# The last half block of a fused attention and MLP kernel: one copy and one store become two of each, on two engines and two queues

## The chip, the cores and the metric

The kernel runs on one core of a Trainium2 chip. The metric is the device time of one execution in microseconds; the median of several executions counts, and lower is better.

## The reference

A state of 32 rows and a sequence of 512 rows attend to each other for each of 8 batches and 8 heads. Both results are joined along the rows, the heads along the columns, and the 4352 rows go through a two-layer MLP with a leaky ReLU.

```python
def _attn_ref(x, state):                      # x 8x8x512x64, state 8x8x32x64
    scores = scale * np.matmul(x, state.transpose(0, 1, 3, 2))
    a = softmax(scores)
    xread = np.matmul(a, state)
    scores2 = scale * np.matmul(state, x.transpose(0, 1, 3, 2))
    a2 = softmax(scores2)
    sread = np.matmul(a2, x)
    return np.concatenate([xread, sread], axis=2)

def _moe_ref(x, w_in, w_out):                 # x 4352x512, w_in 512x2048, w_out 2048x512
    h = x @ w_in
    g = np.maximum(0.01 * h, h)
    return g @ w_out
```

(`softmax` stands here for the written-out maximum, exponential, sum and division of the original.) Inputs and output are fp32; the kernel multiplies in bf16 and accumulates in fp32.

## The kernel before

The kernel works batch by batch. For each batch it computes scores and probabilities, and it folds the state into the first weight matrix, so that the first MLP layer of a batch is one product of probabilities (`aT`) and the folded weights (`M`), 16 blocks of 128 hidden columns for 512 rows (`ff1`, line 429). The second layer is a product of 512 rows x 2048 with 2048 x 512. From batch 2 on, and for half of batch 1, it is done in blocks by a scheme of seven block products instead of eight: sums and differences of blocks are formed on DVE and POOL (`s_sum`, `tw_sum`), and `product` (line 605) multiplies them on TensorE. A block result has 256 rows (two halves of 128, `v` = 0 and 1) and 256 output columns (`HN`).

The products of a batch are normally spread over the next batch's first layer. For the last batch, 7, there is no next one, and its products are written out by hand at the end (lines 1234 to 1276), interleaved with the MLP of the state's rows (`f_product`, `two_product`). The order of the instructions on each engine is that of the source: the pools and the wait placement are automatic, the schedule is manual.

The end of the program is this. After the state rows' last product their results go out in eight stores of 32 rows each, four issued from SP and four from ACT (line 1266). Then product 3 of batch 7 (line 1270), its sum on DVE (`y_add`, line 729) and its store from SP (`y_pair`, line 735). Last comes product 4 in two halves (line 1274): for each half eight matmuls of 128 x 256, which add to what products 1, 6 and 7 left. The two halves lie in two different PSUM tiles (`ppw`, 256 fp32 columns of each are used). The first half is copied to the output tile `ysb` on DVE and the second on ACT (line 1275), and each is stored by SP (line 1276) as 128 rows of 256 fp32 columns, 128 KB. `rows_of(b)[2 + v]` picks every fourth row of the batch's 512 output rows, so each of the 128 rows is a piece of 1 KB in DRAM.

What stands at line 1302 in the profile is the program's closing: SP waits for the completion semaphores of all DMAs, and then the engines meet in a barrier.

Of the kernel before, what the change touches and what calls it, by code (L numbers as in the profile page):

```python
# [9 lines left out]
P = 128  # L10
# [17 lines left out]
def kernel(  # L28
# [9 lines left out]
    nc = tc.nc  # L38
# [14 lines left out]
    VEC, SCA, POO = nc.vector.tensor_copy, nc.scalar.copy, nc.gpsimd.tensor_copy  # L53
# [496 lines left out]
    HN = DM // 2  # L550
# [27 lines left out]
    hTs, sums, prods = {}, {}, {}  # L578
# [26 lines left out]
    def product(b, n, v, j0=0, j1=8):  # L605
        q = prods.setdefault(b, {})
        bank = "x" if n in (1, 6, 7, 4) else "b"
        first = n in (1, 2, 5) and v == 0 and j0 == 0
        if first:
            if b == B - 1 and n == 1:  # L610
                ts = [psum.tile([P, 2, DM], FP32, name="ppw", tag=t, bufs=1) for t in ("sc", "big")]
                q[bank] = [t[:, 0, :HN] for t in ts]
                q["whole", bank] = None
            else:
                t = psum.tile([P, 2, HN], FP32, name=f"pp{bank}", tag="py")
                q[bank] = [t[:, u] for u in range(2)]
                q["whole", bank] = t[:]
        wide = b == B - 1 and n == 1
        q["open", bank] = first or (wide and j0 == 0)
        at = slice(P * v, P * (v + 1))  # L620
        low = slice(HN * 1 + P * v, HN * 1 + P * (v + 1))
        for j in range(j0, j1):
            lhsT = {
                1: lambda: hTs[b][:, j, at],
                2: lambda: hTs[b][:, HJ + j, at],
                4: lambda: hTs[b][:, HJ + j, low],
                3: lambda: sums[b, 4][:, j, at],
                5: lambda: sums[b, 1][:, j, at],
                6: lambda: sums[b, 2][:, j, at],
                7: lambda: sums[b, 3][:, j, at],  # L630
            }[n]()
            nc.tensor.matmul(  # L632
                q[bank][v], lhsT=lhsT, rhs=w_of(n, j), start=q["open", bank] and j == 0,
                stop=j == 7, skip_group_check=True,
            )
# [82 lines left out]
    def y_block(b, u, c):  # L718
        q = prods[b]
        if ("y", u) not in q:  # L720
            q["y", u] = ypool.tile([P, 2, DM], FP32, name="ysb", tag="ysb")
        return q["y", u][:, :, HN * c:HN * (c + 1)]
# [35 lines left out]
    def rows_of(b):  # L758
        return out[b * SROW:b * SROW + S, :].rearrange("(p t) f -> t p f", t=NT)
# [474 lines left out]
    b = B - 1  # L1234
# [37 lines left out]
    y_pair(b, 0, HN, DM)  # L1272
    for v in range(2):
        product(b, 4, v)
        (VEC, SCA)[v](y_block(b, 1, 0)[:, v], prods[b]["x"][v])
        nc.sync.dma_start(rows_of(b)[2 + v][:, :HN], y_block(b, 1, 0)[:, v])


# [28 lines left out]
```

## Time and profile before

| What | us |
|---|---|
| Runs: 202.83, 203.06, 203.06; median | 203.06 |
| Time of the profiled execution | 202.94 |
| Its span, first to last instruction | 201.1 |
| TensorE busy in the span | 194.1 |
| Granted TensorE clock | 1.000 |
| DVE copy of the first half (line 1275), from 197.12 | 0.424 |
| ACT copy of the second half (line 1275), from 198.00 | 0.372 |
| SP's issues of the two last stores (line 1276), from 197.58 and 198.40 | 0.356, 0.345 |
| Last store of 128 KB, from issue to landing | 1.8 |

Times within the span count from its first instruction. PE is TensorE's matmuls, PEld its weight loads, SPq and ACTq the instruction queues of SP and ACT with their DMA issues; "landing" is the arrival of a DMA's completion semaphore. The median of the runs is 0.12 above the profiled execution, whose time holds 1.8 us outside the span.

### The profile page before, as it was taken

To read this page: it belongs to the slowest core of one execution; us is meant where nothing else is said; L and a number is where in the kernel's file an instruction comes from. 1 tells how busy PE (TensorE), PEld (TensorE's weight loads), DVE (VectorE), ACT (ScalarE), POOL (GpSimd) and SP (SyncE) were. 2 spreads that over 40 slices of the span, in tenths; PEclk is the share of its full clock that TensorE was granted. 3 is DMA by queue.
4 is the path that set the end of the run, shared out by engine and by line. 5 is a ranking of instruction groups with operands and counts; after the bars stand their busy time and mean duration, and the time that the engine had idled before them with its cause. 6 is when DMAs were issued, how large, how long until landed. Compare 5 with 4: busy or idle time off the path is not lost.

```text
span 201.1 us, 4590 instructions
## 1 busy us (share of the span) xinstructions
PE 194.1 (96%) x1853; PEld 129.4 (64%) x1880; DVE 161.7 (80%) x243; ACT 143.5 (71%) x273; POOL 62.3 (31%) x67
## 2 busy tenths in 40 slices
PE   6999999999999999999999999999999999999993
PEld 2643534443476767766776677676767777799982
DVE  2866799899998999889987999697999945984712
ACT  3679677888989878777777878777868555757420
POOL 8734180030190274017500670054004600540000
PEclk9999999999999999999999999999999999999999
DMA  6999999896999737843293505220025202210115
GB/s 197 207 206 297 255 261 175 142 345 128 231 220 204 273 46 52 259 197 74 42 265 118 155 3 104 106 108 0 0 100 160 56 3 103 108 47 10 52 37 171
DMA packets 38773, 27.75 MB, mean 138 GB/s; under 512 B 24416, under 2 KB 35808, under 8 KB 38752
## 3 DMA queue, kind: packets, MB, share of 16 engines
q1 hardware_dynamic: 33584, 20.78, 40.7%
q0 software_dynamic: 4832, 6.29, 15.4%
q10 hardware_dynamic: 336, 0.39, 0.8%
q8 instruction: 14, 0.23, 0.5%
q14 instruction: 7, 0.06, 0.1%
HBM read 17.30 MB, written 8.91 MB: 130 GB/s over the span
## 4 chain that ended last, share of the span: by engine, by line
PE 75%; DMA 14%; DVE 3%; ACT 2%; POOL 2%; issue 1%; ACTq 1%; POOLq 0%
PE ph L432 20%; PE ppx L632 18%; PE ppb L632 16%; DMA w_out_bf<-in_moe_w_out_dram 8%; PE ppr L689 6%; DMA w_in_bf<-in_moe_w_in_dram 5%; PE py L537 3%; PE pf L510 3%; PE pm L411 3%; PE ppw L632 3%; PE psr L384 2%; PE pyw L537 2%; DVE tw L576 1%; DMA out_dram<-ysb 1%; POOL w_in_bf L145 1%
## 5 line engine op out<-in xcount | busy, mean ns | idle before, releaser
L437 ACT ACTIVATE hT<-ph 128x512 bf16<-128x512 f32 x112 | 66.4, 603 | 24.0 <-PE ph L432 20.6
L432 PE MATMUL ph<-aT,M 128*128 128x512 bf16 x201 | 60.6, 379 | 0.3
L597 POOL TENSOR_TENSOR S<-hT,S 128x512 bf16<-128x512 bf16 x24 | 32.1, 1359 | 83.1 <-DVE S L597 66.9
L632 PEld LDWEIGHTS <-S 128*128 128x128 bf16 x384 | 37.2, 98 | 12.7 <-issue 0.2
L632 PEld LDWEIGHTS <-hT 128*128 128x128 bf16 x288 | 27.8, 98 | 11.7 <-issue 1.3
L597 DVE TENSOR_TENSOR S<-hT 128x1024 bf16<-128x1024 bf16 x24 | 25.3, 1078 | 2.4 <-ACT hT L437 2.4
L432 PEld LDWEIGHTS <-M 128*128 128x128 bf16 x224 | 20.9, 98 | 9.4 <-issue 3.7
L632 PE MATMUL ppx<-tw,S 128*128 128x256 bf16 x160 | 20.7, 273 | 0.2
L537 PEld LDWEIGHTS <-hT 128*128 128x128 bf16 x96 | 9.1, 98 | 11.6 <-issue 1.3
L537 PE MATMUL py<-w_out_bf,hT 128*128 128x512 bf16 x63 | 15.9, 379 | 0.2
L132 POOL CAST xb<-xl 128x2048 bf16<-128x2048 f32 x5 | 9.5, 1893 | 12.7 <-DMA xl<-in_x_dram 12.7
L425 ACT CAST M<-pm 128x1024 bf16<-128x1024 f32 x12 | 12.2, 1016 | 0.6 <-PE pm L411 0.6
L632 PE MATMUL ppb<-tw,S 128*128 128x256 bf16 x96 | 12.4, 273 | 0.2
L632 PE MATMUL ppb<-w_out_bf,hT 128*128 128x256 bf16 x96 | 12.5, 273 | 0.1
L729 DVE TENSOR_TENSOR ysb<-ppb,s 128x512 f32<-128x512 f32 x12 | 8.3, 688 | 5.3 <-PE ppb L632 5.3
L632 PE MATMUL ppb<-w_out_bf,S 128*128 128x256 bf16 x96 | 12.3, 273 | 0.2
L632 PE MATMUL ppx<-w_out_bf,hT 128*128 128x256 bf16 x80 | 11.2, 273 | 0.1
L337 ACT ACTIVATE e<-sc,mcol 128x512 bf16<-128x512 f32 x16 | 11.1, 697 | 0.0
L632 PE MATMUL ppx<-tw,hT 128*128 128x256 bf16 x80 | 10.4, 273 | 0.1
L289 DVE TRANSPOSE_TENSOR_REDUCE r<-e 128x32 f32<-128x1024 bf16 x7 | 8.7, 1242 | 1.6 <-ACT e L284 1.5
L331 DVE TENSOR_REDUCE mcol<-sc 128x2 f32<-128x1024 f32 x8 | 9.7, 1215 | 0.0
L266 DVE TRANSPOSE_TENSOR_REDUCE mrow<-sc 128x32 f32<-128x1024 f32 x7 | 8.7, 1243 | 0.5 <-PE sc L256 0.5
(150 smaller groups left out, 313.0 us busy)
## 6 DMA issues: line engine op xcount, KB each, us to landing
out_dram<-ysb SPq DMA_DIRECT2D x11, 512.0 KB, 2.6
xl<-in_x_dram SPq DMA_DIRECT2D x5, 1024.0 KB, 6.4
out_dram<-ysb SPq DMA_DIRECT2D x9, 256.0 KB, 4.6
w_in_bf<-in_moe_w_in_dram POOLq DMA_DIRECT2D x4, 512.0 KB, 9.4
xf<-in_x_dram SPq DMA_DIRECT2D x4, 256.0 KB, 3.7
w_out_bf<-in_moe_w_out_dram POOLq DMA_DIRECT2D x4, 256.0 KB, 13.6
x<-in_x_dram POOLq DMA_DIRECT2D x2, 512.0 KB, 14.4
w_out_bf<-in_moe_w_out_dram POOLq DMA_DIRECT2D x2, 512.0 KB, 15.4
```

The source lines that it names most:

```text
L132: nc.gpsimd.tensor_copy(xt[b][:].rearrange("p t h d -> p h t d"), xl[b][:].rearrange("p h (t d) -> p h t d", t=NT),)
L266: nc.vector.tensor_reduce(out=m1[:], in_=flat.rearrange("p (c j) -> p c j", j=NS), axis=AX.X, op=ALU.max, apply_transpose=True,)
L289: nc.vector.tensor_reduce(out=r1[:], in_=e1[:].rearrange("p (c j) -> p c j", j=NS), axis=AX.X, op=ALU.add, apply_transpose=True,)
L331: nc.vector.tensor_reduce(out=a.m2[:], in_=a.sc[:], axis=AX.X, op=ALU.max, negate=True)
L337: nc.scalar.activation(out=a.e2[:, g], in_=a.sc[:, g, :], func=AF.Exp, bias=a.m2[:, g:g + 1], accum_out=a.r2[:, g:g + 1],)
L425: copy(a.M[:, :, cols], pm[:])
L432: nc.tensor.matmul(ph[:], lhsT=a.M[:, g, P * j:P * (j + 1)], rhs=a.aT[:, g, :], start=(g == 0), stop=(g == 1),)
L437: nc.scalar.activation(out=hT[:, j, :], in_=ph[:], func=AF.Prelu, scale=1 / SCALE, alpha=0.01)
L537: nc.tensor.matmul(y.py, lhsT=hT[:, j, P * i:P * (i + 1)], rhs=w_out_bf[:, j, :], start=(j == 0), stop=(j == 15),)
L597: eng.tensor_tensor(out=part(n), in0=in0, in1=in1, op=op)
L632: nc.tensor.matmul(q[bank][v], lhsT=lhsT, rhs=w_of(n, j), start=q["open", bank] and j == 0, stop=j == 7, skip_group_check=True,)
L689: nc.tensor.matmul(q.bank[w], lhsT=lhsT, rhs=w_of(n, j), start=n in (1, 2, 5) and j == 0, stop=j == HJ - 1, skip_group_check=True,)
```

## The change

The first half is treated as before: copied on DVE, stored from SP. The second half's 256 columns are divided: columns 0 to 127 are copied on DVE and stored from SP's queue, columns 128 to 255 are copied on ACT and stored from ACT's queue. Both parts are read from the same PSUM tile. Each store is 64 KB, 128 rows of 512 bytes. Nothing else is altered.

```diff
     for v in range(2):
         product(b, 4, v)
-        (VEC, SCA)[v](y_block(b, 1, 0)[:, v], prods[b]["x"][v])
-        nc.sync.dma_start(rows_of(b)[2 + v][:, :HN], y_block(b, 1, 0)[:, v])
+        y = y_block(b, 1, 0)[:, v]
+        parts = ((VEC, nc.sync, 0, P), (SCA, nc.scalar, P, HN)) if v else ((VEC, nc.sync, 0, HN),)
+        for copy, eng, c0, c1 in parts:
+            copy(y[:, c0:c1], prods[b]["x"][v][:, c0:c1])
+            eng.dma_start(rows_of(b)[2 + v][:, c0:c1], y[:, c0:c1])
```

## The prediction

> **What bounds the kernel now.** I read the page's first part and the chain of waits first. TensorE is busy for 96% of the span and the chain lies on it for three quarters.
>
> ```profile
> span 201.1 us, 4590 instructions
> PE 194.1 (96%) x1853; PEld 129.4 (64%) x1880; DVE 161.7 (80%) x243; ACT 143.5 (71%) x273; POOL 62.3 (31%) x67
> PE 75%; DMA 14%; DVE 3%; ACT 2%; POOL 2%; issue 1%; ACTq 1%; POOLq 0%
> ```
>
> The diff adds no matmul and moves none. Only the end after the last matmul can change, so the next view is the timeline of the last microseconds (start, length, engine, line).
>
> ```profile
> 196.05 1.91 PE L632 MATMUL ppw<-tw,hT 128*128 128x256 bf16 x16
> 196.97 0.39 SPq L735 DMA_DIRECT2D out_dram<-ysb  x1
> 197.12 0.42 DVE L1275 COPY ysb<-ppw 128x256 f32<-128x256 f32 x1 [0.18 <-PE ppw L632]
> 197.58 1.16 SPq L1276 DMA_DIRECT2D out_dram<-ysb  x2
> 198.00 0.37 ACT L1275 COPY ysb<-ppw 128x256 f32<-128x256 f32 x1 [3.12 <-DMA out_dram<-ysb]
> ```
>
> The last matmul ends at 196.05 + 1.91 = 197.96, ACT copies from 198.00 to 198.37, SP issues the last store at 198.40, and the span ends at 201.1. The row puts ACT's wait down to a store of the same moment, but the program's wait is for TensorE, which ended 0.04 before. So 3.1 us of tail follow the last product: 0.4 of copy, 2.7 behind the store's issue. The view of the issues by line and the view of SP's end-of-program instructions split the latter.
>
> ```profile
> L1276 SPq DMA_DIRECT2D out_dram<-ysb x2: 345/350/356, 197.6 to 198.4; - x2
> L1266 ACTq DMA_DIRECT2D out_dram<-ysb x4: 395/441/442, 194.9 to 196.3; - x4
> out_dram<-ysb ACTq DMA_DIRECT2D x4, 64.0 KB, 1.8
> out_dram<-ysb SPq DMA_DIRECT2D x1, 128.0 KB, 1.8
> L1302 SPq EVENT_SEMAPHORE  x9: 28/28/28, 198.8 to 200.2; - x9
> ```
>
> The last store lands 1.8 us after its issue began, at 198.40 + 1.83 = 200.23. SP then passes the last of nine wait instructions, which start at 198.8 to 200.2. These nine are the gate at the program's end: they wait one after another for every DMA semaphore. In narrow windows they start at 198.79, 198.86, 198.92, 198.98, 199.04, 199.33, 199.40, 199.81 and 200.25. The first five had nothing to wait for (their DMAs had landed) and still follow each other by 0.06 to 0.07, (199.04 - 198.79) / 4 = 0.064 us. The sixth, eighth and ninth wait for landings: the 256 KB store, the first 128 KB store, the last one. After the ninth, drains and the closing barrier take 201.13 - 200.25 = 0.88.
>
> **The copy.** The change takes away one ACT copy of 256 columns (0.372) and puts in a DVE and an ACT copy of 128 columns. No row has a DVE copy of 128 fp32 columns out of PSUM. DVE takes 0.424 for 256 and 0.692 for 512 (the row of line 547), so 0.268 per 256 columns and 0.424 - 0.134 = 0.290 for 128; bounds are 0.175 (the 128x16 row of line 831) and 0.424. ACT has a row of that size:
>
> ```profile
> L191 ACT CAST st<-pst x1: 272/272/272, 5.8 to 5.8; 128x128 bf16<-128x128 f32 x1
> ```
>
> The instruction list of the changed program decides how they stand to each other: the DVE copy waits for TensorE, the ACT copy waits for DVE's count after that copy, and not for TensorE. The two copies of one PSUM bank are in line, not at once. DVE is free (its copy of the first half ends at 197.55), so it runs from 198.00 to 198.29; a hand-over takes some 0.03 (TensorE's end at 197.96 to ACT's start at 198.00, ACT's end at 198.37 to SP's issue at 198.40); ACT runs from 198.32 to 198.59. Before, all 256 columns were out at 198.37: the split is 0.22 late.
>
> The Trainium skill, in PSUM — Partial Sum Buffer, section PSUM bank collisions raise a hardware error, holds that two engines may not access one bank and quadrant together, reads against reads included. By that rule the wait is needed; no run here shows a collision. Were the copies side by side, the sum below would be 0.3 smaller.
>
> **The stores.** The last store of 128 KB becomes two of 64 KB. SP's own (128 rows of 512 B) is issued after the DVE copy, at 198.32 and not 198.40, and is off the path. ACT's is issued after its copy, at 198.59 + 0.03 = 198.62. Nothing is queued on ACT behind it, and its queue has been empty since 198.03 (the fourth L1266 store, 196.30 + 1.73). ACT's issue takes 0.40 to 0.44 against SP's 0.35. The windows view gives the DMA engines a share of 0.91 at 198.50 to 199.00, 0.27 at 199.00 to 199.20, and 0.96 at 199.40 to 199.60 (the last store): they are free again when the new stores' packets come, from 199.2 on.
>
> How long does 64 KB in 512 B pieces take to land? No row has it. The nearest are ACT's four stores of 64 KB (2 KB pieces), 1.7 to 1.9, and SP's of 128 KB, 1.8. Half the bytes may save up to half of the 0.45 us in which the last store's packets ran; the longer issue costs 0.09. I take 1.8, with 1.6 (fastest L1266 store) and 2.0 (slowest) as bounds. ACT's half is landed at 200.42 (200.22 to 200.62), against 200.23 before.
>
> The Trainium skill, in DMA: Bandwidth & Descriptors, section Issuing engines are not separate DMA queues, says that issuing from two engines saves only the issuing time, since the transfers share the same DMA engines. By that rule the second queue could save 0.35 here at most. It saves 0.05, because ACT's store is ready at 198.62 and SP would be free at 198.32 + 0.35 = 198.67; ACT's longer issue takes that back.
>
> **The gate at the end.** This is the dearest term and the diff does not show it. Each DMA issued from SP or ACT takes the next of eight completion semaphores in turn, and SP's nine end waits go through these in their fixed order, the first instruction having none of them. Before, the last store had the eighth: it was the last thing SP waited for, and everything else was passed during its flight. One store more means that ACT's store takes the first semaphore. In the changed program's list the second of the nine instructions waits for it. SP reaches it at about 198.77, stands there until 200.42, and only then passes seven more, which have all landed (the first half's store, the latest other, stood at 199.81; SP's half lands near 198.32 + 1.8 = 200.12). Seven of them at 0.064 are 0.45. This cost is at most 0.48 (0.069 each) and at least nothing, if passed waits should run closer.
>
> **Sum.** Old end of the gate: 200.25. New: 200.42 + 0.015 (landing to passing, as before) + 0.45 = 200.88. The difference is +0.63: 0.22 from the later issue (198.62 for 198.40), less 0.03 of landing (1.80 for 1.83), plus 0.45 from the gate, rounded. What hid those seven waits was the last store's flight; that cover is gone. With landing 1.6 to 2.0 it is +0.43 to +0.83. The profiled execution took 202.94, 1.8 more than its span; that gives 203.57. The runs' median is 203.06 (202.83 to 203.06), which gives 203.69. I forecast 203.6, between the two.
>
> **Rivals.**
> *The gate costs nothing* (passed waits overlap): 203.06 + 0.18 = 203.2, no change. For it: each wait instruction is only 28 ns long. Against: the five passed waits before have the 0.064 spacing without anything to wait for. Chance 0.06.
> *The change does what it says*, and the copies run side by side: ACT ends at 198.27, its store lands at 198.30 + 1.8 = 200.10, and the gate ends at 200.57, +0.32: 203.35, read as no change. Against: the wait in the instruction list. Chance 0.04.
> *A store's time goes with its bytes* (the other side, not slower): the 64 KB land in half of 1.83, 0.92 after 198.62, at 199.54. Then ACT's store no longer ends last; SP passes the waits up to the seventh by 199.87, the first half's store having landed by 199.81, and the last at 200.12 at the latest, or below 200 if SP's half gains too: -0.15 to -0.35, 202.7 to 202.9. It decides once landing takes below 1.17 us. Against: the page's 64 KB stores take 1.6 to 2.0, as long as 128 KB. Chance 0.04, half of it read as faster by the scatter of the runs (202.83 to 203.06), half as no change.
> *The two last stores collide*: 512 B pieces run at the cost of larger ones and two queues share the engines, landing 2.0 or later as the slowest SP store did beside ACT's: +0.83 and more, 203.9. For it: the 32-row stores issued from both queues at once landed up to 0.4 apart. Against: the stores are issued 0.3 apart and each needs some 0.2 us of packets. Chance 0.07.
>
> **How the numbers follow.** The forecast has 0.79. A measurement of this kernel tells about 0.2%, 0.41 us, from no change. Some 0.04 of the forecast (landing at its short bound, or the scatter of 0.23 among the runs) reads as no change. Slower: 0.75 + 0.07 = 0.82; no change: 0.04 + 0.06 + 0.04 + 0.02 = 0.16; faster: 0.02. The range is the forecast's own bounds from the lowest run (202.83 + 0.43 = 203.26) to the median with the long landing (203.06 + 0.83 = 203.89), rounded out to 203.25 and 203.95; it takes in the second and the fourth rival.
>
> **What would show it.** In the changed profile the DVE copy starts at 198.0 and the ACT copy at 198.3, after it. Of SP's nine end waits one has started by 198.8, the second starts at 200.4 and the other seven follow within 0.45. If the ACT copy starts at 198.0, the copies are side by side; if the last wait starts within 0.1 of the landing of ACT's store, the gate term is wrong; if that store lands before 199.8, the landing is.

## The result and the profile after

The changed kernel takes 203.56 us (median of 14 runs, 203.20 to 204.49) against 203.06 (14 runs, 202.66 to 203.78): a ratio of 1.003 with a 95% interval of 1.0016 to 1.0044, so half a microsecond slower. One of the runs with one store more below (207.43 us) and two of those with four more (207.07 and 206.47) had a lower granted clock, 0.992, and are left out of the medians and ratios. The profiled execution took 203.46 with a span of 201.7; that of before took 202.94 with 201.1.

The page of the changed kernel, its first part:

```profile
span 201.7 us, 4620 instructions
PE 195.8 (97%) x1880; PEld 129.4 (64%) x1880; DVE 161.2 (80%) x244; ACT 143.2 (71%) x273; POOL 62.4 (31%) x67
```

TensorE shows 27 matmuls more only because the trace of before misses as many records (1853 against 1880 weight loads in both). The timeline of the end (start, length, engine, line, operation, and in brackets what the engine waited for):

```profile
196.13 1.91 PE L632 MATMUL ppw<-tw,hT 128*128 128x256 bf16 x16
197.66 1.08 SPq L1279 DMA_DIRECT2D out_dram<-ysb  x2
198.08 0.29 DVE L1278 COPY ysb<-ppw 128x128 f32<-128x128 f32 x1 [0.45 <-PE ppw L632]
198.40 0.27 ACT L1278 COPY ysb<-ppw 128x128 f32<-128x128 f32 x1 [3.44 <-DVE ysb L1278]
198.70 0.36 ACTq L1279 DMA_DIRECT2D out_dram<-ysb  x1
```

The last matmul ends at 198.04. The two copies run one after the other: ACT sat idle for 3.44 us and what ended the wait is DVE's copy of the other columns. Copying ends at 198.67, 0.63 after the last matmul; before it was 0.41. ACT issues its store at 198.70. The issues of the last three stores, with the median time from issue to landing:

```profile
out_dram<-ysb SPq DMA_DIRECT2D x1, 128.0 KB, 2.2
out_dram<-ysb SPq DMA_DIRECT2D x1, 64.0 KB, 1.7
out_dram<-ysb ACTq DMA_DIRECT2D x1, 64.0 KB, 1.7
```

So ACT's half is landed 1.65 later, at 200.35. Now the end waits of SP in the changed kernel, first in the view of what SP's queue waited for (total, times, longest), then its wait instructions up to that landing and behind it (count, shortest, median and longest in ns, first and last start):

```profile
SPq L1305 <- DMA out_dram<-ysb: 1.5, 1, 1.5
```

```profile
L1305 SPq EVENT_SEMAPHORE  x1: 17/17/17, 198.8 to 198.8; - x1
...
L1305 SPq EVENT_SEMAPHORE  x8: 28/28/28, 200.4 to 200.8; - x8
```

And the first of these views for the kernel before:

```profile
SPq L1302 <- DMA out_dram<-ysb: 1.0, 3, 0.4
```

Before, SP went through its nine waits while the stores landed, held up three times for 0.4 at most. After, it passes one wait, stands 1.5 us at the second, and then goes through eight (the one that held it and seven that had nothing to wait for) from 200.36 to 200.79. That walk of 0.43 us lies behind the last landing and in front of the closing barrier, which takes 0.88 in both kernels.

In the sections below all times of the tail count from the end of the last matmul, since that end itself moves from profile to profile (197.62 to 198.78 in the profiles read below of kernels with the matmuls of before). Two points matter: when the last store is landed, and when the last of SP's end waits starts.

| Kernel | last store issued | landed | last end wait |
|---|---|---|---|
| before | 0.43 | 2.27 | 2.29 |
| after | 0.66 | 2.31 | 2.75 |

The difference is 0.47 us: 0.22 from the later issue, -0.19 from the shorter landing, 0.43 from the gate. The span grew by 0.54, since the last matmul also ended 0.08 later in this profile.

### The profile page after: what moved, and what is told of

It reads as the page before. It is cut to its first block, busy times and chain, and to the rows that moved or that the text cites. A ratio compares the mean times of both kernels' runs of the same rounds, so it can differ in the third digit from the quotient of the medians.

```text
span 201.7 us, 4620 instructions
## 1 busy us (share of the span) xinstructions
PE 195.8 (97%) x1880; PEld 129.4 (64%) x1880; DVE 161.2 (80%) x244; ACT 143.2 (71%) x273; POOL 62.4 (31%) x67
## 4 chain that ended last, share of the span: by engine, by line
PE 78%; DMA 13%; DVE 4%; POOL 2%; ACT 1%; issue 0%; POOLq 0%; ACTq 0%
PE ph L432 22%; PE ppx L632 17%; PE ppb L632 16%; DMA w_out_bf<-in_moe_w_out_dram 8%; PE ppr L689 6%; DMA w_in_bf<-in_moe_w_in_dram 5%; PE ppw L632 3%; PE py L537 3%; PE pf L510 3%; PE pm L411 3%; PE psr L384 2%; PE pyw L537 2%; DVE tw L576 1%; POOL w_in_bf L145 1%; PE sc L256 1%; DVE sh L274 1%
## 5 line engine op out<-in xcount | busy, mean ns | idle before, releaser
L432 PE MATMUL ph<-aT,M 128*128 128x512 bf16 x224 | 65.3, 379 | 0.1
```

Source lines behind the costliest of these rows:

```text
L432: nc.tensor.matmul(ph[:], lhsT=a.M[:, g, P * j:P * (j + 1)], rhs=a.aT[:, g, :], start=(g == 0), stop=(g == 1),)
```

## The experiments

**One store more, nothing else.** From the kernel before; the store of batch 7's first block half is cut into two. The expectations put this store some 15 us ahead of the end; in the trace of before it is issued at 179.40, 21.7 ahead of it.

```diff
-            y_pair(b, 0, 0, HN)
+            for v in range(2):
+                nc.sync.dma_start(rows_of(b)[v][:, :HN], y_block(b, 0, 0)[:, v])
```

> The kernel before, with one store more about 15 us ahead of the end: the store of batch 7's first block half is cut into two. Copies and last stores are those of before; only the completion semaphores move on by one, so that the last store has the first of the eight. From the last matmul's end to the last of SP's end waits it is 2.29 us before and 2.75 after. Theory (the gate costs 7 waits of 0.062): 2.72, and a time 0.43 us over before's. Rival (the time was lost in the copies in line and the stores, the gate is free): 2.29 and before's time.

203.29 us against 202.90, a ratio of 1.0027 (1.0017 to 1.0037). The last store lands at 2.28, as before, and the last end wait starts at 2.73 (the theory said 2.72). SP's end waits in this kernel, the one ahead of the landing and those from it on:

```profile
L1303 SPq EVENT_SEMAPHORE  x1: 28/28/28, 198.4 to 198.4; - x1
...
L1303 SPq EVENT_SEMAPHORE  x8: 28/28/28, 199.9 to 200.3; - x8
```

It is the picture of the changed kernel, one wait and then eight, with the copies and the last stores of before. A store cut far from the end, with nothing else changed, brings the tail to 2.73 where the whole change brings it to 2.75.

**The changed kernel with the gate hidden again.** The same early store goes out from POOL, whose DMAs count on other semaphores; ACT's last store then has the eighth again.

```diff
-            y_pair(b, 0, 0, HN)
+            nc.gpsimd.dma_start(pair_rows(b, 0)[:, :, :HN], prods[b]["y", 0][:, :, :HN])
```

> The changed kernel, with the store of batch 7's first block half, some 15 us ahead of the end, issued from POOL instead of SP. POOL's stores count on other semaphores, so those of SP and ACT move back by one and ACT's last store has the eighth again. Copies in line and split stores stay. Theory: the gate's 0.43 us goes, last matmul to last end wait 2.75 - 0.43 = 2.32, time equal to before's within 0.1 us. Rival (gate free, copies and stores cost it all): 2.75 and still 0.5 us over before's.

202.97 us against 202.90, a ratio of 1.0003 (0.9993 to 1.0012). Landing at 2.31 as in the changed kernel, last end wait at 2.33 against its 2.75. All nine of SP's end waits, from the first to the last start, in one view:

```profile
L1305 SPq EVENT_SEMAPHORE  x9: 17/28/28, 198.8 to 200.4; - x9
```

With the gate hidden, the copies in line and the split store cost 0.04 us of tail over before, less than the runs can tell.

**The control for the moved store**: the same edit in the kernel before.

> The kernel before, with only the store of batch 7's first block half issued from POOL. The last store then has the seventh semaphore; one wait follows its own. It is the control for the runs in which this store was moved. Theory: 2.29 + 0.06 = 2.35, a time within 0.1 us of before's. Rival (the moved store itself is what brought the changed kernel back to before's time): clearly under before's time, by 0.2 us or more.

The last store lands at 2.27, SP passes it at 2.29, and the last end wait starts at 2.35, one step of 0.06 later. The time is 203.05 against 202.99, a ratio of 1.0019 (1.0007 to 1.0032). It is not under before's, so the move is not what brought the changed kernel back. That the ratio is more than 0.06 us would make is left open; the medians are 0.06 apart.

**Four stores more.** The early store cut into five, so that four waits follow the last store's.

```diff
-            y_pair(b, 0, 0, HN)
+            for i in range(5):
+                lo, hi = (0, 32, 64, 96, 112, 128)[i:i + 2]
+                nc.sync.dma_start(pair_rows(b, 0)[lo:hi, :, :HN], prods[b]["y", 0][lo:hi, :, :HN])
```

> The kernel before, with the store of batch 7's first block half, some 15 us ahead of the end, cut into five. The last store then has the fourth of the eight semaphores and four waits follow its own. Theory (each wait behind the last landing costs 0.062): last matmul to last end wait 2.29 + 0.25 = 2.54. Rival (one more wait behind it costs the same whatever the number): 2.72 as with seven; or nothing, 2.29.

203.36 us against 202.99, a ratio of 1.0016 (0.9998 to 1.0035). Its profiled execution is the one of 207.07 us, so the tail is read from another execution of the same kernel:

> The kernel with the store of batch 7's first block half cut into five, once more for its profile. Theory: the last store lands 2.27 after the last matmul, as before, and four waits of 0.06 follow: last matmul to last end wait 2.53. Rival (one more wait behind it costs the same whatever the number): 2.72.

It took 203.16 beside 203.25 before, which says nothing either way; the tail does. The last store lands at 2.32, 0.05 later than before's, and the last end wait starts at 2.58, 0.24 after SP passed the landing. SP's end waits from the landing on:

```profile
L1304 SPq EVENT_SEMAPHORE  x5: 28/28/28, 200.2 to 200.5; - x5
```

Five instructions, the one that waited and four that did not. The walk behind the landing is thus 0.06 for one wait (the control), 0.24 for four and 0.43 for seven: 0.061 each.

**One copy, two stores.** From the changed kernel; ACT copies all 256 columns of the last half, and both stores wait for that.

```diff
-        parts = ((VEC, nc.sync, 0, P), (SCA, nc.scalar, P, HN)) if v else ((VEC, nc.sync, 0, HN),)
-        for copy, eng, c0, c1 in parts:
-            copy(y[:, c0:c1], prods[b]["x"][v][:, c0:c1])
+        (VEC, SCA)[v](y, prods[b]["x"][v])
+        for eng, c0, c1 in ((nc.sync, 0, P), (nc.scalar, P, HN)) if v else ((nc.sync, 0, HN),):
             eng.dma_start(rows_of(b)[2 + v][:, c0:c1], y[:, c0:c1])
```

> The changed kernel, with the last half's 256 columns copied by ACT in one instruction as before, and the two stores of 64 KB kept, one from SP and one from ACT, both waiting for that copy. The gate is as in the changed kernel. Theory: both stores are issued 0.40 after ACT's start instead of 0.64, so last matmul to last end wait 2.75 - 0.22 = 2.53, a time 0.24 over before's. Rival (the copies in line cost nothing, because the two stores share the DMA engines and the pair lands as late as one of 128 KB): 2.29 + 0.43 = 2.72.

203.43 us against 202.90, a ratio of 1.0029 (1.0015 to 1.0043). The theory fell. The stores were issued at 0.44, 0.22 sooner than ACT's in the changed kernel, and the last end wait still started at 2.79, later than its 2.75 and past the rival's 2.72. The timeline of this kernel and its issues with their times to landing:

```profile
197.95 0.37 ACT L1276 COPY ysb<-ppw 128x256 f32<-128x256 f32 x1 [3.12 <-DMA out_dram<-ysb]
198.35 0.34 SPq L1278 DMA_DIRECT2D out_dram<-ysb  x1
198.35 0.37 ACTq L1278 DMA_DIRECT2D out_dram<-ysb  x1
```

```profile
out_dram<-ysb SPq DMA_DIRECT2D x1, 64.0 KB, 1.9
out_dram<-ysb ACTq DMA_DIRECT2D x1, 64.0 KB, 2.1
```

Issued together, the two halves land 1.9 and 2.1 after issue instead of 1.7 and 1.7 when they were 0.3 apart. SP's half has the first semaphore here, so the gate's walk of 0.43 starts at its landing, 2.35, and covers ACT's at 2.51.

**One copy, two stores, gate hidden**: the last edit and the store from POOL together.

> Both edits together: ACT copies 256 columns in one, two stores of 64 KB from two queues, and one earlier store issued from POOL, so that SP's last store has the eighth semaphore. Theory: the gate is hidden again and 64 KB land 0.17 sooner than 128 KB (1.67 for 1.84): last matmul to last end wait 2.29 - 0.17 = 2.12, a time 0.17 us under before's. Rival (stores issued together share the DMA engines and land as one of 128 KB): 2.29, before's time.

203.15 us against 202.90, a ratio of 1.0008 (0.9998 to 1.0018). It did not beat before: ACT's half landed at 2.46, and the last end wait started at 2.54, 0.25 later than before's. Here ACT's half has the seventh semaphore and SP's the eighth, so one wait of 0.06 still follows the last landing; the other 0.19 is the landing itself. Two stores of 64 KB at once are later than one of 128 KB (2.27).

**Half of it alone.** The run with one copy and two stores without SP's half: the left 128 columns of the last half are left out of the output.

```diff
-        for eng, c0, c1 in ((nc.sync, 0, P), (nc.scalar, P, HN)) if v else ((nc.sync, 0, HN),):
+        for eng, c0, c1 in ((nc.scalar, P, HN),) if v else ((nc.sync, 0, HN),):
```

> ACT copies the last half's 256 columns in one, and only the right 128 columns are stored, 64 KB from ACT; the left 128 columns of that half are left out of the output. ACT's store has the eighth semaphore. It is the run with one copy and two stores without SP's half. Theory (two stores issued together hold each other up): issued at 0.44 after the last matmul, landed 1.65 later, last matmul to last end wait 2.10. Rival (it is ACT's queue, or 512 B pieces, at that moment): 2.46 to 2.54 as with both.

It was run once, 202.75 us beside 202.97. The view of its last issues:

```profile
out_dram<-ysb SPq DMA_DIRECT2D x1, 128.0 KB, 2.2
out_dram<-ysb ACTq DMA_DIRECT2D x1, 64.0 KB, 1.6
```

The same store from the same queue, issued at the same 0.44, lands at 2.08 when SP's is not there, and at 2.46 to 2.51 when it is. It is the company that costs, not ACT's queue or the pieces of 512 B.

**Copies side by side.** From the changed kernel; the right 128 columns of the last half are accumulated in another PSUM tile.

```diff
-                q[bank] = [t[:, 0, :HN] for t in ts]
+                q[bank] = [ts[0][:, 0, :HN], [ts[1][:, 0, :P], ts[0][:, 1, :P]]]
...
-            nc.tensor.matmul(
-                q[bank][v], lhsT=lhsT, rhs=w_of(n, j), start=q["open", bank] and j == 0,
-                stop=j == 7, skip_group_check=True,
-            )
+            to, w = q[bank][v], w_of(n, j)
+            for p, r in zip(to, (w[:, :P], w[:, P:])) if isinstance(to, list) else ((to, w),):
+                nc.tensor.matmul(
+                    p, lhsT=lhsT, rhs=r, start=q["open", bank] and j == 0,
+                    stop=j == 7, skip_group_check=True,
+                )
...
```

The rest of the diff makes the readers of that half follow.

> The changed kernel, with the right 128 columns of the last half accumulated in another PSUM tile (matmuls of 128 columns for that half, 32 more in all, so TensorE works some us longer; only the tail is read). The ACT copy no longer waits for the DVE copy. ACT's store has the eighth semaphore and SP's the first, so the gate stays. Both copies start at 0.04 after the last matmul and both stores are issued at 0.34 to 0.36. Theory (two stores issued together land later, as in the run with one copy and two stores, 1.9 and 2.08 after issue): last matmul to last end wait 0.355 + 1.91 + 0.43 = 2.70, so that side by side copies gain only 0.05 on the changed kernel's 2.75. Rival (64 KB land 1.65 after issue, as ACT's store did in the changed kernel): 0.355 + 1.65 + 0.43 = 2.44, a gain of 0.31.

The time, 204.06 against 202.99, holds the 32 added matmuls and is not compared. The tail in the timeline, and the issues with their times to landing:

```profile
198.67 0.29 DVE L1281 COPY ysb<-ppw 128x128 f32<-128x128 f32 x1 [1.03 <-PE ppw L634]
198.73 0.27 ACT L1281 COPY ysb<-ppw 128x128 f32<-128x128 f32 x1 [3.76 <-DMA out_dram<-ysb]
198.99 0.35 SPq L1282 DMA_DIRECT2D out_dram<-ysb  x1
199.03 0.36 ACTq L1282 DMA_DIRECT2D out_dram<-ysb  x1
```

```profile
out_dram<-ysb SPq DMA_DIRECT2D x1, 64.0 KB, 1.8
out_dram<-ysb ACTq DMA_DIRECT2D x1, 64.0 KB, 1.9
```

ACT starts 0.06 after DVE, while DVE is still copying: the wait for DVE came from the shared PSUM tile. SP's half lands at 2.10 and ACT's at 2.27; the last end wait starts at 2.55, between the theory's 2.70 and the rival's 2.44. SP's end waits from its half's landing on:

```profile
L1308 SPq EVENT_SEMAPHORE  x8: 27/28/28, 200.8 to 201.2; - x8
```

That is 0.20 off the changed kernel's tail, but the copies are little of it. In this kernel SP's half has the first semaphore and ACT's the eighth, so the walk of 0.43 starts at SP's landing, 2.10, and covers ACT's. The later landing itself moved only from 2.31 to 2.27; an estimate from these rows for the changed kernel's order of waits is 2.27 + 0.02 + 0.43 = 2.72, only 0.03 off its 2.75. And 2.27 is also the landing of the single 128 KB store before. Even with copies side by side the store is not in sooner; the 0.1 us gained at the copy goes to two stores that hold each other up.

**The store cut by rows.** One ACT copy, 64 rows of 1 KB from SP and 64 from ACT, with the store from POOL. The edit is against the kernel before.

```diff
-            y_pair(b, 0, 0, HN)
+            nc.gpsimd.dma_start(pair_rows(b, 0)[:, :, :HN], prods[b]["y", 0][:, :, :HN])
...
-        (VEC, SCA)[v](y_block(b, 1, 0)[:, v], prods[b]["x"][v])
-        nc.sync.dma_start(rows_of(b)[2 + v][:, :HN], y_block(b, 1, 0)[:, v])
+        y = y_block(b, 1, 0)[:, v]
+        (VEC, SCA)[v](y, prods[b]["x"][v])
+        for eng, p0, p1 in ((nc.sync, 0, 64), (nc.scalar, 64, P)) if v else ((nc.sync, 0, P),):
+            eng.dma_start(rows_of(b)[2 + v][p0:p1, :HN], y[p0:p1])
```

> One ACT copy of 256 columns as before, its store divided by rows and not by columns: 64 rows of 1 KB from SP and 64 from ACT, issued together, and the earlier store from POOL, so that the gate is hidden. Half as many pieces as with the cut by columns. Theory (two stores issued together land late, whatever their pieces): last matmul to last end wait 2.45 to 2.54, as with the cut by columns (2.54). Rival (the 512 B pieces are what costs): 2.27 or less, a time equal to before's or under it.

203.56 us against 202.99, a ratio of 1.003 (1.0012 to 1.0048), and neither expectation held: the last end wait started at 2.97. Each issue took 0.56 to 0.58 instead of 0.35, and the halves landed 2.2 and 2.5 after it. So one half was tried by itself, from the kernel before; the last half's other 64 rows are left out of the output.

```diff
-        (VEC, SCA)[v](y_block(b, 1, 0)[:, v], prods[b]["x"][v])
-        nc.sync.dma_start(rows_of(b)[2 + v][:, :HN], y_block(b, 1, 0)[:, v])
+        y = y_block(b, 1, 0)[:, v]
+        (VEC, SCA)[v](y, prods[b]["x"][v])
+        for p1 in (64,) if v else (P,):
+            nc.sync.dma_start(rows_of(b)[2 + v][:p1, :HN], y[:p1])
```

> The kernel before, with only the first 64 of the last half's 128 rows stored, 64 KB in pieces of 1 KB from SP; the other 64 rows of that half are left out of the output. It is the run with the store divided by rows without ACT's half. Theory (the two issues at once made each other last 0.56 to 0.58 and land 2.1 or more after): issue 0.345, landed 1.65 after it, last matmul to last end wait 2.10. Rival (a store of 64 rows takes that long to issue by itself): issue 0.56, 2.3 or more.

It was run once, 202.98 us beside 202.97. The timeline row, in which 1.38 spans two issues, and the store's time to landing:

```profile
197.30 1.38 SPq L1278 DMA_DIRECT2D out_dram<-ysb  x2
```

```profile
out_dram<-ysb SPq DMA_DIRECT2D x1, 64.0 KB, 2.2
```

Alone it takes 0.57 to issue and lands 2.16 after (last end wait 2.61), where twice the rows take 0.345 and 1.84. The rival holds: the long issue belongs to the store of 64 rows. Its packets also start 1.2 us after the issue began instead of 0.8. Why, no run here tells.

## Why the prediction was right

*The place.* Only the tail after the last matmul could change, and only it did, but for the 0.08 us by which the end of TensorE's work wanders.

*The copies.* Predicted in line, with ACT's store issued 0.22 late; measured 0.66 against 0.43, 0.22. The DVE copy was put at 0.290 from the line through the 256- and 512-column rows and took 0.291; ACT's was put at 0.272 and took 0.266. That the cause is the shared PSUM tile was argued; the run with two tiles shows it. The rule of the Trainium skill (PSUM — Partial Sum Buffer, section PSUM bank collisions raise a hardware error) fits that wait; no run here tried two readers of one bank at once.

*The stores.* This is the mis-sized term. The prediction took 1.80 for 64 KB on ACT's queue, the middle of the L1266 stores and 0.03 under 128 KB. It took 1.65, inside its bounds of 1.6 to 2.0. The prediction leaned on issues of 0.40 to 0.44 in the L1266 row; here ACT's issue took 0.357, 0.012 more than SP's. And half the bytes did save time: the last store's packets of 512 B took 27 ns each against 46 for 1 KB, and all 128 of them 0.36 us against 0.51. The landing makes 0.15 of the 0.16 by which the forecast difference (+0.63) stands above the measured one (+0.47); the rest is the gate.

*The gate.* Predicted 7 x 0.064 = 0.45; measured 0.43, 0.061 each, and shown by itself with one store more (0.43 for seven), four more (0.24) and moved back (gone). It is 0.43 of the 0.47 us; without it the changed kernel is at a ratio of 1.0003 (0.9993 to 1.0012).

*The sum.* 203.6 forecast, 203.56 measured; +0.63 forecast, +0.47 in the tail, +0.50 between the medians. That the time itself came out within 0.04 is partly luck: 203.6 lies near the sum from the profiled execution of before, whose time was 0.12 under the median, and that made up for most of the landing's 0.15; from the median the same sum gave 203.69, 0.13 too high.

*The rivals.* "The gate costs nothing" fell with the first run. "The change does what it says" was priced at +0.32 with the gate; the run with two tiles gives 2.55 - 2.29 = +0.26, for a reason that the prediction did not have: it put the landing at 1.8 for want of a nearer row, and the two stores issued together do take 1.8 and 1.9. The order of the waits that this price assumed, ACT's store first, was not the one of that run either. By the Trainium skill (DMA: Bandwidth & Descriptors, section Issuing engines are not separate DMA queues) a second queue saves the issuing time at most; the runs with two stores at once go further and show a loss: with one copy for both and one store from POOL, the last landing is at 2.46 where that of the single store is at 2.27. "A store's time goes with its bytes": a store of half the bytes lands 0.19 sooner, not 0.92. "The last two stores collide" did not happen at 0.3 apart, and did when they were issued together.

No version tried that stores the whole output beats the kernel before.

## What to carry to other kernels

Look at what the program waits for at its end and in which order: the transfers that land late should be waited for late, because every wait behind such a landing is paid in full, 0.06 us here. It is not enough that the very last is waited for last: with one copy and two stores it was, and the walk of 0.43 was paid all the same, since the other half landed only 0.17 earlier and stood first. One store more, 22 us ahead of the end, turned that order here, and moving one to POOL turned it back, so a change that touches the number of DMAs carries a term that its diff does not show, up to 0.43 us in this kernel. And splitting the last store over two queues is worth only as much as the landing moves: here half the bytes landed only 0.19 of 1.84 us sooner, and two halves issued together landed no sooner than the whole.

## What the hardware showed that was not expected

Two 64 KB stores issued at the same moment from SP and ACT land 1.9 and 2.1 us after issue, where the same ACT store alone lands in 1.64, and one of 128 KB in 1.84. Their packets finish 1.86 after the last matmul, only 0.07 later than the packets of the single store (1.79), but the last completion follows its packets after 0.65 instead of 0.48.

A store of 64 rows of 1 KB takes 0.57 to issue and 2.16 to land, longer in both than a store of 128 such rows (0.345 and 1.84), alone or in company.
